# A routed attention and expert kernel: the first turn's weight sums ahead of its rows in the last pair

## The chip, the cores and the metric

The kernel runs on one core of one Trainium2 chip. The metric is device time in microseconds (us), the median of several runs. TensorE is called PE, VectorE DVE, ScalarE ACT, GpSimd POOL and SyncE SP, as the profile does.

## The reference

Two blocks follow each other. The first is a clustered attention over 4 batches, 8 heads, 768 positions and 64 values a head: each query and key is given to the nearest of 16 centroids of its head, and a query sees only the keys of its own cluster.

```python
q_assign = np.argmax(np.einsum('bhsd,hcd->bhsc', q_n, c_n), axis=-1)
k_assign = np.argmax(np.einsum('bhsd,hcd->bhsc', k_n, c_n), axis=-1)
mask = q_assign[:, :, :, None] == k_assign[:, :, None, :]
scores = np.where(mask, scale * np.matmul(q, k.transpose(0, 1, 3, 2)), -1000000000.0)
attn = np.exp(scores - max) / sum          # cut
attn_out = np.matmul(attn, v)
```

The result, 3072 rows of 512, goes through a layer of 8 experts, one expert for each row:

```python
logits = x @ w_gate
expert_idx = np.argmax(logits, axis=1)
gate_w = probs[np.arange(N), expert_idx]   # probs: softmax of logits
for e in range(E):                         # rows of expert e
    h = np.maximum(x_e @ w1[e], 0.0)       # w1[e]: 512 x 1024
    y_e = h @ w2[e]                        # w2[e]: 1024 x 512
out = gate_w[:, None] * y
```

## The kernel before

**Attention, in pairs of heads.** There are 16 pairs, 0 to 15, four to a batch (HP is 4). A pair has 12 units: two halves of the queries (h) by six blocks of keys (j). In each unit `score` (L433) puts scores in PSUM, first q against k, then the cluster masks MQ and MK as a second matmul into the same place; ACT takes the exponential into a tile A (L445), and for j over 0 DVE adds the A tiles to acc (`add_up`, L451). After the units, `attend` (L457) multiplies A by v, and ACT copies the result to oT (L464).

**Work between the units.** The order on every engine is the order of the program; it is written by hand. `at_pair(n, u, f, ...)` hangs a call of f behind unit u of pair n. Unit 12 is between the two halves of `attend`, unit 13 is after them. In this way hang:

- the masks of the next pair: `similar` (PE, L291), then on DVE `assign0`, `assign1` and `assign2` (L302 to L327, ending in ohT), then `place` on ACT (four writes of mk at L340, four of mq at L337), at unit 11;
- the sums of the pair before: `sum_up` (PE, L480) and `weights_of` (DVE, L489 to L504, the gate logits lgb) at unit 2, `rows` (DVE, L510) and `store` (SP, L517, to x_rows) at unit 4;
- the routing of a finished batch: `gate`, `gate_exp`, `gate_sum`, `choose`, `count` (PE, L592), `number` (DVE), and the scatter of positions by POOL to tokens_of (L607).

**Turns of the expert layer.** A turn is up to 448 rows of one expert. There are 10; the first two (EARLY, 288 rows each) take rows of the first three batches, and are got ready while the last batch is still in attention. The steps of turn 0 are:

- `rank_first` (DVE, L645 to L650): 13 small instructions, which choose the experts of turns 0 and 1;
- `first_turns` (SP): reads the experts' numbers, fetches `sf`, the tokens and their factors (`places`, L712 and L716), and then w1 and w2 of turn 0 (L97 and L105);
- `indices` (DVE, L728 and L729) for turns 0 and 1, `gather` (POOL, L738, three indirect DMAs to xg), `weigh` (DVE, L755, and SP's DMAs to turn_rows, L761), `take` (SP, L771, four DMAs to xs), `turn_rows` (DVE, a transpose to xT, L780), `x_sums` (DVE, four sums xc of xT, at L789);
- `w1_sums` (DVE, the four sums a of w1, also recorded at L789).

The last two are the sums of Strassen's scheme (Winograd's form), in which a 2 x 2 block product takes 7 products.

**Layer 1 of turn 0.** `layer1` (matmuls at L968) does 7 products for each of two halves of the hidden blocks, 14 in all. The first takes a block of w1 and xT, the second A[2] and X[2], the third A[1] and X[1], the fourth blocks of w1 and xT, the fifth A[0] and X[0], the seventh A[3]. Behind each product is a hook, 0 to 13, from which calls in `h1` run. In turn 0 these are the last pair's `sum_up` and `weights_of` and the routing of the last batch. The add that makes h (DVE, L926) reads the fifth product, and the seventh product writes into the same bank. `layer2` (L1088 here) follows.

```python
at_pair(n, 2, sum_up, n - 1)
at_pair(n, 4, rows, n - 1)
at_pair(n, 4, store, n - 1)
```

Of the kernel before, what the change touches and what calls it, by code (L numbers as in the profile page):

```python
# [33 lines left out]
def kernel(  # L34
# [11 lines left out]
    nc = tc.nc  # L46
    B, H, S, D = q.shape
# [120 lines left out]
    with tc.manual_schedule(), ExitStack() as actx:  # L168
# [596 lines left out]
        def take(s):  # L765

            g = GR[s]
            T, C = g["T"], g["C"]
            g["xs"] = xp.tile([P, T_MAX // Q4, P], F32, name="xs")
            for r in range(HP):  # L770
                nc.sync.dma_start(  # L771
                    out=g["xs"][Q4 * r : Q4 * (r + 1), 0:C, :],
                    in_=g_d[s][0:T, P * r : P * (r + 1)].rearrange("(c t) d -> t c d", t=Q4),
                )
# [49 lines left out]
        def at_pair(n, u, f, *a):  # L824
            AT.setdefault((n, u), []).append(lambda: f(*a))
# [8 lines left out]
        for b in range(B - 1):  # L834
            n = HP * (b + 1)
# [8 lines left out]
            at_pair(n, 2, weights_of, n - 1)  # L844
        n = HP * (B - 1)
        slots = range(len(EARLY))
        at_pair(n + 1, 4, rank_first)

        def first_turns():
            for s in slots:  # L850
# [3 lines left out]
            GR[0]["w1"] = fetch1(GR[0]["e"], wa)  # L854
            GR[0]["w2"] = fetch2(GR[0]["e"], wa)

        at_pair(n + 1, 6, first_turns)
        for s in slots:
            at_pair(n + 1, 13, indices, s)
        at_pair(n + 2, 6, gather, 0)  # L860
        at_pair(n + 2, 13, weigh, 0)
        at_pair(n + 3, 1, take, 0)
        at_pair(n + 3, 4, turn_rows, 0)
        at_pair(n + 3, 6, x_sums, 0)
        at_pair(n + 3, 9, w1_sums, 0, (2, 1), nc.vector)
        at_pair(n + 3, 13, w1_sums, 0, (0, 3), nc.vector)

        def between(n, u):
            for f in AT.pop((n, u), ()):
# [24 lines left out]
    with tc.manual_schedule(), ExitStack() as ectx:  # L894
# [125 lines left out]
        def pairs_of(s):  # L1020


            return GR[s]["T"] // (2 * P) if s else 0

        def h_sums(s):

            g = GR[s]
            g["H"] = []
            for p in range(pairs_of(s)):
                c0 = 2 * P * p  # L1030
                h = g["h"]
                a11, a21 = h[:, 0:4, c0 : c0 + P], h[:, 0:4, c0 + P : c0 + 2 * P]
                a12, a22 = h[:, 4:8, c0 : c0 + P], h[:, 4:8, c0 + P : c0 + 2 * P]
                t = [hpool.tile([P, 4, P], F32, name=f"hs{i}") for i in range(4)]
                V = nc.vector
                strassen(V, t[2], a11, a21, ALU.subtract)
                strassen(V, t[0], a21, a22, ALU.add)
                strassen(V, t[1], t[0], a11, ALU.subtract)
                strassen(V, t[3], a12, t[1], ALU.subtract)
                g["H"].append((a11, a12, a22, t))  # L1040
# [116 lines left out]
        n = NPAIR  # L1157
        last = NS - 1

        def first_weights(s):  # L1160
            if s >= len(EARLY):
                expert(s)
            GR[s]["w1"] = fetch1(GR[s]["e"], (wa, wb)[s % 2])

        def second_weights(s):
            GR[s]["w2"] = fetch2(GR[s]["e"], (wa, wb)[s % 2])

        for s in range(NS):
            h1, h2 = {}, {}

            def at(d, i, f, *a):
                d.setdefault(i, []).append(lambda: f(*a))

            if s == 0:
                at(h1, 2, sum_up, n - 1)
                at(h1, 2, weights_of, n - 1)
                at(h1, 3, gate, B - 1)
                at(h1, 3, gate_exp, B - 1)
                at(h1, 5, gate_sum, B - 1)
                at(h1, 5, choose, B - 1)  # L1180
                at(h1, 8, count, B - 1)
                at(h1, 9, number, B - 1)
                at(h1, 11, rows, n - 1)
                at(h1, 11, store, n - 1)
                at(h1, 12, rank_all)
                at(h2, 0, rank_rest)
                at(h2, 3, places, 2)
                at(h2, 3, first_weights, 2)
                at(h2, 5, places, 3)
                at(h2, 7, indices, 2)  # L1190
                at(h2, 7, gather, 2)
            if s == 3:
                at(h1, 12, ask)
                at(h2, 4, answer)
            if s < last:
                if s == 0:
                    first_weights(1)
                elif s > 1:
                    take(s + 1)
                if s == 1:  # L1200
                    at(h1, 6, weigh, 2)
                    at(h1, 7, take, 2)
                    at(h1, 8, second_weights, 2)
                else:
                    second_weights(s + 1)
                if 0 < s <= last - 2:
                    at(h2, 0, first_weights, s + 2)

                if 0 < s <= last - 3:
                    at(h2, 1, places, s + 3)  # L1210

                if s == 0:
                    when = ((h2, 1), (h2, 2), (h2, 5), (h2, 6), (h2, 7), (h2, 7))
                elif s == 1:
                    when = ((h1, 9), (h1, 12), (h2, 2), (h2, 3), (h2, 6), (h2, 6))
                else:
                    when = ((h1, 9), (h1, 10), (h2, 1), (h2, 2), (h2, 2), (h2, 5))
                if GR[s + 1]["T"] >= 2 * P:
                    for (h, i), f, a in zip(when, (w1_sums,) * 4 + (w2_sums,) * 2, (2, 1, 0, 3, 2, 0)):
                        at(h, i, f, s + 1, (a,), nc.vector)  # L1220
                at(h2, 1 if s == 1 else 3, turn_rows, s + 1)
                if GR[s + 1]["T"] >= 2 * P:
                    at(h2, 1 if s == 1 else 4, x_sums, s + 1)
            if s == 0:
                at(h1, 2, gather, 1)
                at(h1, 8, weigh, 1, slice(0, 1))
                at(h1, 11, weigh, 1, slice(1, 2))
                at(h1, 12, weigh, 1, slice(2, 3))
                at(h1, 12, take, 1)
            elif s + 2 <= last:  # L1230
                at(h1, 5 if s == 2 else 4, indices, s + 2)
                at(h1, 5 if s == 2 else 4, gather, s + 2)
                at(h2, 6 if s == 1 else 4, weigh, s + 2)
            if pairs_of(s):
                at(h1, 4, w2_sums, s, (1,), nc.vector)

                at(h1, 5 if s == 1 else 6, w2_sums, s, (3,), nc.vector)
            if s == last - 1:

                at(h1, 4, nc.gpsimd.drain)  # L1240
            (layer1 if GR[s]["T"] >= 2 * P else few_columns)(s, h1)
            h_sums(s)
            layer2(s, h2)
# [271 lines left out]
```

## Time and profile before

| what | value |
| --- | --- |
| median of 3 runs | 660.87 us (659.3 to 662.08) |
| the profiled execution | 659.27 us, span 657.5 us |
| PE busy | 644.2 us, 98% of the span |
| DVE busy | 490.0 us, 75% |
| ACT busy | 338.8 us, 52% |
| POOL busy | 130.8 us, 20% |
| granted PE clock | 0.998 |
| first score matmul of pair 13, 14, 15 | 268.96, 288.84, 310.37 us |
| first matmul of the seeds before layer 1 of turn 0 | 329.47 us |
| first matmul of layer 2 of turn 0 | 347.20 us |

The profile is of one execution. Times of the trace count from the start of the span. An instruction of the timeline is given as start, duration, engine, line, operation, what it writes and reads, and in brackets how long the engine stood idle before it and for what. A matmul's end is modelled, so its start is the firmer number.

### The profile page before, as it was taken

The page shows a single profiled execution, that of the slowest core. Times are in us where ns is not written, and L with a number is a line of the kernel's source. Part 1 is how long each engine was busy: PE and PEld are TensorE (multiplying, and loading weights), DVE is VectorE, ACT ScalarE, POOL GpSimd, SP SyncE. Part 2 cuts the span into 40 slices and gives each one's busy share as a digit, 9 for nine tenths or more (in the row PEclk, how much of TensorE's full clock was granted, in tenths as well). Part 3 has the DMA queues.
Part 4 walks back from the last instruction along what each step waited for, and adds up shares of the span by engine and source line. Part 5 has one row for each costly group of instructions (what it writes and reads, how often), then busy time and mean ns, then how long its engine had stood idle before and what let it go on. Part 6 is the DMA issues. An engine that isn't in the chain of part 4 may idle for free.

```text
span 657.5 us, 11491 instructions
## 1 busy us (share of the span) xinstructions
PE 644.2 (98%) x4252; PEld 423.3 (64%) x4252; DVE 490.0 (75%) x845; ACT 338.8 (52%) x584; POOL 130.8 (20%) x166
## 2 busy tenths in 40 slices
PE   8999999999999999999999999999999999999996
PEld 4444544455444454544484979989797987869773
DVE  6988888998889988989887997888869365572300
ACT  4677878768878777867532333333231331323210
POOL 4500000022000300041103522324240422140010
PEclk9999999999999999999999999999999999999999
DMA  7663455443355433347475587776684835614010
GB/s 150 150 120 68 76 94 97 72 80 68 73 97 98 74 76 72 72 132 227 117 273 156 187 314 264 252 275 211 249 307 170 273 138 165 233 74 173 7 49 19
DMA packets 189760, 95.38 MB, mean 145 GB/s; under 512 B 152895, under 2 KB 171839, under 8 KB 188416
## 3 DMA queue, kind: packets, MB, share of 16 engines
q1 hardware_dynamic: 184624, 81.56, 45.2%
q0 software_dynamic: 4928, 12.97, 6.1%
q8 instruction: 35, 0.57, 0.4%
q14 instruction: 29, 0.24, 0.1%
q10 hardware_dynamic: 144, 0.03, 0.0%
HBM read 74.10 MB, written 20.70 MB: 144 GB/s over the span
## 4 chain that ended last, share of the span: by engine, by line
PE 80%; issue 10%; DVE 5%; POOL 2%; ACT 1%; DMA 1%; POOLq 0%; DVEq 0%; ACTq 0%
PE sps L433 20%; PE mps L457 16%; PE bank L968 10%; PE sbank L968 8%; PE bank L1069 7%; PE bank L1088 7%; PE sbank L1069 6%; PE mps L480 2%; PE mps L291 1%; PE bank L937 1%; DMA xg<-x_rows,gi 1%; DVE xT L780 1%; POOL tokens_of L607 1%; DVE acc L451 1%; DVE a L789 1%
## 5 line engine op out<-in xcount | busy, mean ns | idle before, releaser
L445 ACT ACTIVATE A<-sps 128x768 f32<-128x768 f32 x192 | 152.1, 814 | 30.0 <-PE sps L433 29.4
L433 PE MATMUL sps<-qT,kT 64*128 64x384 f32 x768 | 158.9, 492 | 0.0
L451 DVE TENSOR_TENSOR acc<-acc,A 128x768 f32<-128x768 f32 x128 | 121.4, 948 | 11.4 <-ACT A L445 2.9
L457 PE MATMUL mps<-A,v_in 128*64 128x384 f32 x768 | 127.4, 488 | 0.0
L433 PEld LDWEIGHTS sps<-qT,kT 64*128 64x128 f32 x768 | 66.8, 187 | 52.2 <-issue 48.4
L457 PEld LDWEIGHTS mps<-A,v_in 128*64 128x64 f32 x768 | 53.7, 137 | 70.6 <-issue 62.9
L1043 POOL DMA_INDIRECT out_dram<-z,si x30 | 47.7, 1590 | 196.0 <-DVE z L926 167.2
L607 POOL DMA_INDIRECT tokens_of<-tg,pos_i x24 | 27.5, 1147 | 270.5 <-DVE pos_i L605 264.4
L433 PE MATMUL sps<-mq,mk 64*128 64x384 bf16 x384 | 64.9, 323 | 3.1 <-ACT mq L337 1.3
L1088 PE MATMUL bank<-w,h 128*128 128x512 f32 (+2 forms) x224 | 64.4, 596 | 0.0
L340 ACT ACTIVATE mk<-ohT,kscn,ksc 32x384 bf16<-32x384 bf16 x60 | 42.0, 700 | 40.5 <-DVE ohT L327 39.7
L968 PE MATMUL bank<-xT,w 128*128 128x144 f32 (+4 forms) x288 | 47.7, 309 | 0.0
L738 POOL DMA_INDIRECT xg<-x_rows,gi x30 | 38.4, 1280 | 47.0 <-DVE si L729 16.4
L968 PE MATMUL sbank<-xc,a 128*128 128x144 f32 (+4 forms) x288 | 47.7, 309 | 0.0
L1088 PEld LDWEIGHTS bank<-w,h 128*128 128x128 f32 (+2 forms) x224 | 24.6, 151 | 32.5 <-issue 32.3
L968 PEld LDWEIGHTS bank<-xT,w 128*128 128x128 f32 x288 | 43.8, 190 | 2.6 <-issue 2.2
L451 DVE TENSOR_TENSOR acc<-A 128x768 f32<-128x768 f32 x32 | 30.4, 952 | 19.2 <-ACT A L445 19.1
L968 PEld LDWEIGHTS sbank<-xc,a 128*128 128x128 f32 x288 | 43.4, 190 | 0.0
L926 DVE TENSOR_TENSOR h<-sbank,p 128x288 f32<-128x288 f32 (+4 forms) x18 | 9.2, 514 | 45.7 <-PE sbank L968 45.5
L433 PEld LDWEIGHTS <-mk 64*128 64x128 bf16 x384 | 19.9, 94 | 29.0 <-DVE mk L383 2.6
L986 ACT ACTIVATE h<-h 128x288 f32<-128x288 f32 (+4 forms) x36 | 17.6, 488 | 38.1 <-DVE h L926 38.1
L755 DVE TENSOR_TENSOR xw<-xg,sf 128x256 f32<-128x256 f32 (+2 forms) x60 | 32.8, 606 | 0.9 <-DMA xg<-x_rows,gi 0.6
(216 smaller groups left out, 900.5 us busy)
## 6 DMA issues: line engine op xcount, KB each, us to landing
w<-in_moe_w_dram SPq DMA_DIRECT2D x20, 2048.0 KB, 10.7
v_in<-in_v_dram SPq DMA_DIRECT2D x32, 192.0 KB, 2.5
x_rows<-x SPq DMA_DIRECT2D x64, 96.0 KB, 2.4
turn_rows<-xw SPq DMA_DIRECT2D x23, 256.0 KB, 2.0
q_in<-in_q_dram SPq DMA_DIRECT2D x60, 96.0 KB, 3.2
k_in<-in_k_dram SPq DMA_DIRECT2D x60, 96.0 KB, 3.2
xs<-turn_rows SPq DMA_DIRECT2D x16, 144.0 KB, 2.8
xs<-turn_rows SPq DMA_DIRECT2D x8, 208.0 KB, 4.2
```

The costliest lines, as they stand in the source:

```text
L340: nc.scalar.activation(dst, src, AF.Identity, bias=less, scale=big)
L433: nc.tensor.matmul(SP[n, h, j][:, a, 0:HS], lhsT=kt[rows, j * P : (j + 1) * P], rhs=qt[rows, h * HS : (h + 1) * HS], start=first, stop=not ...
L445: nc.scalar.activation(A[n, h, j], ps[:, :, 0:HS], AF.Exp, scale=D**-0.5)
L451: nc.vector.tensor_tensor(ACC[n, h], first, A[n, h, j], op=ALU.add)
L457: nc.tensor.matmul(O[n, h][D * a : D * (a + 1), 0:HS], lhsT=VIN[n][:, a, j, :], rhs=A[n, h, j][:, a, :], start=(j == 0), stop=(j == NQ - 1),)
L607: ins = nc.gpsimd.indirect_dma_start(out=t_d[:, :], out_offset=bass.IndirectOffsetOnAxis(ap=pos_i[:, i : i + 1], axis=0), in_=tg[:, b, i, ...
L738: nc.gpsimd.indirect_dma_start(out=xg[0:m], out_offset=None, in_=x_d[0:rows_in, :], in_offset=bass.IndirectOffsetOnAxis(ap=g["gi"][0:m, j ...
L755: nc.vector.tensor_tensor(xw[0:m, :, :, d2 * a : d2 * (a + 1)], xg[0:m].rearrange("p (r a d b) -> p a r b d", r=HP, a=2, b=DB)[:, a], g["s ...
L968: nc.tensor.matmul(ps[:, f * T2 : (f + 1) * T2], lhsT=w[:, k, (2 * j + f) * P : (2 * j + f + 1) * P], rhs=x[:, k, :], start=first and f + ...
L1043: ins = nc.gpsimd.indirect_dma_start(out=out[:, :], out_offset=bass.IndirectOffsetOnAxis(ap=GR[s]["si"][0:rows, j : j + 1], axis=0), in_=z ...
L1069: nc.tensor.matmul(ps[:, 0:H], lhsT=x[:, k, :], rhs=y[:, k, :], start=first and k == 0, stop=k == 3, skip_group_check=not first,)
L1088: nc.tensor.matmul(ps[i * m : (i + 1) * m, :], lhsT=h[:, f, j * P : j * P + m], rhs=w[:, f, :], start=(k == 0), stop=(k == FB // n - 1),)
```

## The change

n is 12 here, so that n + 1 to n + 3 are pairs 13 to 15. `rank_first` and `first_turns` go from units 4 and 6 of pair 13 to its units 9 and 11. `indices` goes from behind pair 13 to unit 2 of pair 14. `weigh` and `take` go from behind pair 14 and unit 1 of pair 15 to units 11 and 13 of pair 14. In pair 15 the four weight sums, which ran in two groups at units 9 and 13, run one each at units 1 to 4; `turn_rows` and `x_sums` go from units 4 and 6 to 6 and 7. In layer 1 of turn 0, `sum_up`, `weights_of`, `gate` and `gate_exp` move one hook later. No instruction is added or removed.

```diff
-        at_pair(n + 1, 4, rank_first)
+        at_pair(n + 1, 9, rank_first)
...
-        at_pair(n + 1, 6, first_turns)
+        at_pair(n + 1, 11, first_turns)
         for s in slots:
-            at_pair(n + 1, 13, indices, s)
+            at_pair(n + 2, 2, indices, s)
         at_pair(n + 2, 6, gather, 0)
-        at_pair(n + 2, 13, weigh, 0)
-        at_pair(n + 3, 1, take, 0)
-        at_pair(n + 3, 4, turn_rows, 0)
-        at_pair(n + 3, 6, x_sums, 0)
-        at_pair(n + 3, 9, w1_sums, 0, (2, 1), nc.vector)
-        at_pair(n + 3, 13, w1_sums, 0, (0, 3), nc.vector)
+        at_pair(n + 2, 11, weigh, 0)
+        at_pair(n + 2, 13, take, 0)
+
+        for u, i in enumerate((2, 1, 0, 3)):
+            at_pair(n + 3, u + 1, w1_sums, 0, (i,), nc.vector)
+        at_pair(n + 3, 6, turn_rows, 0)
+        at_pair(n + 3, 7, x_sums, 0)
...
-                at(h1, 2, sum_up, n - 1)
-                at(h1, 2, weights_of, n - 1)
-                at(h1, 3, gate, B - 1)
-                at(h1, 3, gate_exp, B - 1)
+                at(h1, 3, sum_up, n - 1)
+                at(h1, 3, weights_of, n - 1)
+                at(h1, 4, gate, B - 1)
+                at(h1, 4, gate_exp, B - 1)
```

## The prediction

> **What bounds the kernel now.** The page's first part says that TensorE (PE) is busy 98% of the span, so only time in which PE stands or is slowed can be won.
>
> ```profile
> PE 644.2 (98%) x4252; PEld 423.3 (64%) x4252; DVE 490.0 (75%) x845; ACT 338.8 (52%) x584; POOL 130.8 (20%) x166
> ```
>
> Next I cut the span at the first score matmul of pairs 12 to 15 and at the first matmul of layer 1 and layer 2 of turn 0 (found in PE's timeline), and asked for busy time by stretch: pair 13, pair 14, pair 15, layer 1 of turn 0, layer 2 of turn 0.
>
> ```profile
> 268.96:288.84 19.88, 19.88 (x156) 9.77 (x154) 18.21 (x45) 11.90 (x18) 6.77 (x6) 1.00 0.21 45
> 288.84:310.37 21.53, 20.21 (x154) 9.89 (x152) 19.49 (x37) 17.47 (x27) 4.58 (x4) 1.00 0.76 254
> 310.37:329.47 19.10, 19.10 (x146) 9.41 (x145) 15.88 (x27) 11.70 (x17) 2.26 (x2) 1.00 0.40 100
> 329.47:347.20 17.73, 16.76 (x144) 15.13 (x143) 14.69 (x37) 6.08 (x16) 2.04 (x3) 1.00 0.68 253
> 347.20:362.98 15.78, 15.78 (x50) 6.41 (x49) 11.27 (x31) 3.07 (x6) 5.52 (x6) 1.00 0.68 199
> ```
>
> The first figure is the stretch, then PE, weight loads, VectorE (DVE), ScalarE (ACT), GpSimd. Pair 15 has no "similar" matmuls, which take 0.65 in pair 14, so pair 14 should last 19.10 + 0.65 = 19.75: it loses **1.78 us**. Layer 1 is 14 products of 0.98, the seeds 0.66, the summing 1.02 and the count 0.05, 15.45 in all: it loses **2.28 us**. The waits of PE name both places (first the pairs, then layer 1):
>
> ```profile
> PE sps L433 <- ACT mq L337: 1.3, 2, 1.1
> PE sbank L968 <- DVE h L926: 0.7, 1, 0.7
> PE mps L592 <- DVE last L586: 0.2, 1, 0.2
> ```
>
> After 360 us PE's waits sum to 1.5 us, so time won here should be kept. Last, the timeline behind the first wait:
>
> ```profile
> 279.60 0.11 DVE L645 TENSOR_TENSOR c<-run,first_place 1x8 f32<-1x8 f32 x1
> 281.70 0.16 DVE L650 CAST xe<-xe_f 1x2 int32<-1x2 f32 x1
> 286.82 0.58 DVE L327 STREAM_TRANSPOSE ohT<-oh 128x384 bf16<-128x384 bf16 x1
> 287.43 2.85 ACT L340 ACTIVATE mk<-ohT,kscn,ksc 32x384 bf16<-32x384 bf16 x4 [5.56 <-DVE ohT L327]
> 290.86 0.32 PE L433 MATMUL sps<-mq,mk 64*128 64x384 bf16 x1 [1.10 <-ACT mq L337]
> ```
>
> rank_first stands in DVE's queue ahead of the mask chain (sim to ohT) of pair 14; ohT ends at 287.4, ACT writes four mk and then mq, and PE wants the second mq at 289.6 and gets it at 291.39. And behind the second loss, in pair 15 and layer 1:
>
> ```profile
> 322.41 1.38 DVE L780 STREAM_TRANSPOSE xT<-xs 128x1152 f32<-128x1152 f32 x1 [2.48 <-DMA xs<-turn_rows]
> 333.59 1.22 DVE L789 TENSOR_TENSOR a<-w 128x1024 f32<-128x1024 f32 x1
> 334.73 1.22 DVE L789 TENSOR_TENSOR a<-w,a 128x1024 f32<-128x1024 f32 x1
> 335.86 0.38 DVE L489 STREAM_TRANSPOSE slt<-mps 128x192 f32<-128x192 f32 x1
> 338.24 0.46 DVE L926 TENSOR_TENSOR h<-sbank,p 128x288 f32<-128x288 f32 x1 [0.22 <-PE bank L968]
> ```
>
> DVE stands 2.48 us for the turn's rows, and is then late: its last adds end at 333.7, while PE's summing (L480) has begun at 333.16, and the first layer-1 add comes at 338.24, for which the last product waits.
>
> [...] the trace has 1.22 us for a weight sum[...] layer 1 shows 0.97 us idle where 2.28 is lost, so I use starts, and DVE's queue is its program order. [...] gathers issued while w1 and w2 were in flight landed after 6.2 to 8.1 us, later ones after 4.1 to 5.0.
>
> **The change, part by part.** Times are on the scale of the trace.
>
> *rank_first from unit 4 to unit 9 of pair 13.* 13 small DVE instructions, 279.60 to 281.78, 2.18 us, go behind the mask chain. ohT then ends at 285.2 and ACT has the second mq at 289.15, ahead of PE's 289.6: the wait goes, **gain 1.78**. Late next is DVE itself: the last adds of pair 13 still end at 291.3, where pair 14's summing begins at 291.5, so 0 to 0.2 may return.
>
> *What follows from a later rank.* It ends at 289.33 instead of 281.86. SP's loads of the expert numbers were at 282.5, behind the store of rows; SP spent 2.55 us to its first sf read, waited 2.4 us for tokens_of (then done), and took 3.43 us from the first sf to the second weight fetch. So sf issues at 291.95 to 294.35, w1 at 294.9 and w2 at 295.4, 4.5 us later than now. Nothing else stands in SP's queue in between: the rows of pair 12 go before, those of pair 13 come at 299. With the landings of the trace, sf is there at 296.0 (1.5 to 1.8 us), w1 at 302 (7.4), w2 at 311.5 (16.1).
>
> *indices from (13, 13) to (14, 2).* Eight instructions, 0.63 us, enter DVE's pair 14. DVE comes to them at 293.1 + 3.3 (two acc, the weights_of) = 296.4, so 0.4 us of cover remains over sf. A wait there would hold every acc and the next mask chain behind it. The chain ends at 297.0 + 8.4 = 305.4; ACT gives the second mq at 309.3, PE wants it at 308.6 + 0.75 = 309.3: no cover left, 0 to 0.3.
>
> *gather, weigh, take.* The gathers keep their place; POOL gets gi at 296.5, 3 us later than now, and issues at 296.6 to 300. With 6.2 to 8.1 us they land by 308; weigh reaches DVE at 297.0 + 12.3 = 309.3. Cover 1.3 us. weigh at unit 11 and take at 13 stand in the queues of DVE and SP exactly where they stood, since pair 14 prepares no pair 16: nothing, and their seven DMAs move with weigh, 1.0 us earlier.
>
> *Weight sums first, rows later, in pair 15.* The same nine DVE instructions. Four sums of 1.2 us now fill the wait for xs (landed at 321.4), w1 having landed at 302. DVE's list from 312.6: ten acc at 0.98, four sums 4.85, weights_of 1.35, x 0.95, xT 1.35, xc 1.75, ends at 332.6 at most (332.2 by single starts), xT at 325.6 and xc at 328.2. PE starts layer 1 at 327.7 (329.47 - 1.78), wants X[2] at 329.3 and all of xc by 330.3: in time.
>
> *sum_up and weights_of one hook later, gate too.* PE reaches the summing after four products, at 332.3, with the adds done: the 0.6 lost there goes. DVE runs weights_of at 333.4 to 334.9 and the add for h at once, so the 0.9 at the last product goes. But the count keeps its hook, 5 products after the summing instead of 6. From the end of the summing, 333.4, to "last" I sum 1.5 + 0.5 + 0.7 + 1.05 (Exp, u2, the second add) + 2.2 = 5.95 us, where PE needs 5.0: a wait of up to 0.95 where there is 0.2 to 0.4. Layer 1 thus gains 0.9 by this sum and 2.2 at most if all waits vanish. The rows of that sum were taken with DVE behind; I take the middle, **1.6**.
>
> Sum: 1.78 + 1.6 = 3.4, bounds 0 and 4.0. The profiled execution took 659.27 us (span 657.5 and 1.8 around it), so 655.9; the median of the runs shown, 660.87, is 1.6 above it, so **657.5** on that scale. Their scatter is 659.3 to 662.08.
>
> **Rivals.**
> 1. *The count becomes the wait.* Gain 1.78 + 0.9, with 0 to 0.5 back from the thin covers: 2.2 to 2.7, or 658.2 to 658.7. For it: the latencies are measured. Against: the chain may shorten where DVE isn't behind.
> 2. *The turn's data come late (slower).* If the gathers queue behind the 4 MB of weights, they land after w2's 311.5 and weigh holds DVE from 309.3, with the ten acc of pair 15 and the summing behind it. Every us after 309.3 is a us of layer 1. Slower than before from a landing after 312.7 on, and by over 0.5% from 316; at 317 the time is 657.5 + 7.7 = 665.2. For it: 4.5 us later weights. Against: the gathers of now landed in the midst of the same 4 MB.
> 3. *No real move.* Parts of the edit leave the queues as they are (weigh, take). But rank_first and the sums do change places in DVE's queue; left without gain only if pair 14's wait returns at pair 15 (cover 0): 660.9.
>
> **How the numbers follow.** A difference of 0.5%, 3.3 us, is about what a measurement of this kernel can tell from no change. Both losses go: 0.52, faster, 657.5, own range 656.5 to 657.6. Rivals 1 and 3: 0.36, within 0.5%. Rival 2: 0.12. The range runs from the bound of 4.0 with the scatter of the runs, 654.8, to rival 3 with the same, 661.6.
>
> **What would show it.** In pair 14 no PE wait for mq, and 19.8 us from start to start; rank_first after ohT; the gi instructions without a DMA wait at about 296.4; xT without one; layer 1 at 16.1 us (16.8 under rival 1, with a wait of the count, L592, on "last"). Wrong: a DVE wait on sf or xg of over 1 us, a PE wait for mq in pair 15, or layer 1 over 17.5.

## The result and the profile after

| | before | after |
| --- | --- | --- |
| median (11 runs each) | 660.87 us (659.3 to 662.08) | 658.29 us (656.73 to 659.77) |
| the profiled execution | 659.27 us, span 657.5 | 657.44 us, span 655.7 |

The ratio of after to before is 0.9967, with a 95% interval of 0.9956 to 0.9979: 2.2 us gained (1.4 to 2.9), where 3.4 was forecast. In the changed program the lines behind the edit are one higher (L926 is L927, L968 is L969).

The busy time by stretch, cut at the same matmuls (pair 14, pair 15, layer 1 of turn 0), has the stretch and its length first, then PE, weight loads, DVE, ACT and POOL:

```profile
288.37:308.64 20.27, 20.27 (x154) 9.79 (x152) 18.72 (x39) 14.77 (x22) 4.47 (x4) 1.00 0.70 251
308.64:327.74 19.10, 19.10 (x147) 9.41 (x145) 18.77 (x29) 12.15 (x18) 2.27 (x2) 1.00 0.53 121
327.74:344.36 16.62, 16.03 (x143) 14.99 (x142) 11.83 (x35) 5.99 (x16) 2.05 (x3) 1.00 0.72 270
```

Pair 14 lost 1.26 us of its 21.53, pair 15 is as long as before with DVE 2.9 us busier in it, layer 1 lost 1.11 us of its 17.73. PE's waits from pair 12 to the start of turn 1 now are one line. The wait for mq and the one for the add of h are gone; the one at the count has grown from 0.2:

```profile
PE mps L592 <- DVE last L586: 0.6, 1, 0.6
```

The timeline of the kernel after, from pair 13 to layer 1, has the start, the duration and, in brackets, the idle time before. These are the lines that answer to those shown of before:

```profile
284.13 0.58 DVE L327 STREAM_TRANSPOSE ohT<-oh 128x384 bf16<-128x384 bf16 x1
284.75 2.85 ACT L340 ACTIVATE mk<-ohT,kscn,ksc 32x384 bf16<-32x384 bf16 x4 [3.35 <-DVE ohT L327]
286.54 0.15 DVE L645 TENSOR_TENSOR c<-run,first_place 1x8 f32<-1x8 f32 x1
291.52 0.94 DVE L277 STREAM_TRANSPOSE kT<-k_in 128x768 f32<-128x768 f32 x1
292.51 0.84 PE L291 MATMUL mps<-kT,cT 128*32 128x384 f32 x4
296.74 0.15 DVE L728 SCALAR_TENSOR_TENSOR gi<-sf 32x1 int32<-32x1 f32 x1 [0.62 <-DMA sf<-tokens_of]
323.66 1.37 DVE L780 STREAM_TRANSPOSE xT<-xs 128x1152 f32<-128x1152 f32 x1
333.66 0.38 DVE L489 STREAM_TRANSPOSE slt<-mps 128x192 f32<-128x192 f32 x1 [2.01 <-PE mps L480]
335.02 0.45 DVE L927 TENSOR_TENSOR h<-sbank,p 128x288 f32<-128x288 f32 x1
339.10 0.17 DVE L586 CAST last<-pr 128x8 bf16<-128x8 f32 x1
```

ohT comes 2.2 us earlier against PE and rank_first starts behind it. xT waits for nothing. DVE now stands ready for the summing (2.01 us idle) where before it was late. Two lines were not in the forecast: PE's similar takes kT only at 292.51, just as DVE has turned it, and the last gi stands 0.62 us for sf.

Against the first matmul of pair 14 the kernel after is 2.37 us ahead at the first matmul of layer 2 of turn 0. It does not keep all of it: it gives back 0.40 in layer 2 of turn 2 and 0.48 in layer 1 of turn 3, and at the end of the span 1.36 is left.

### The profile page after: what moved, and what is told of

Read it like the earlier page. It is cut to its first block, busy times and chain, and to the rows that moved or that the text cites. A ratio compares the mean times of both kernels' runs of the same rounds, so it can differ in the third digit from the quotient of the medians.

```text
span 655.7 us, 11490 instructions
## 1 busy us (share of the span) xinstructions
PE 643.5 (98%) x4252; PEld 423.0 (65%) x4252; DVE 489.5 (75%) x845; ACT 338.3 (52%) x584; POOL 133.0 (20%) x166
## 4 chain that ended last, share of the span: by engine, by line
PE 94%; DVE 4%; issue 0%; ACT 0%; POOL 0%; POOLq 0%; DVEq 0%; ACTq 0%
PE sps L433 24%; PE mps L457 19%; PE bank L969 12%; PE bank L1089 10%; PE sbank L969 9%; PE bank L1070 7%; PE sbank L1070 6%; PE mps L480 3%; PE mps L291 2%; PE bank L938 1%; DVE xT L780 1%; DVE a L789 1%; DVE v L789 1%; PE sps L356 0%; PE sps L226 0%
## 5 line engine op out<-in xcount | busy, mean ns | idle before, releaser
L738 POOL DMA_INDIRECT xg<-x_rows,gi x30 | 40.3, 1343 | 45.8 <-DVE si L729 16.5
L969 PE MATMUL sbank<-xc,a 128*128 128x144 f32 (+4 forms) x288 | 47.9, 309 | 0.2 <-ACT sbank L1002 0.2
L969 PE MATMUL bank<-xT,w 128*128 128x144 f32 (+4 forms) x288 | 47.6, 308 | 0.0
L969 PEld LDWEIGHTS bank<-xT,w 128*128 128x128 f32 x288 | 43.8, 190 | 2.3 <-issue 1.9
L969 PEld LDWEIGHTS sbank<-xc,a 128*128 128x128 f32 x288 | 43.3, 190 | 0.7 <-ACT sbank L1002 0.4
L927 DVE TENSOR_TENSOR h<-sbank,p 128x288 f32<-128x288 f32 (+4 forms) x18 | 9.2, 513 | 45.3 <-PE sbank L969 43.9
```

What stands on the lines that cost most here:

```text
L738: nc.gpsimd.indirect_dma_start(out=xg[0:m], out_offset=None, in_=x_d[0:rows_in, :], in_offset=bass.IndirectOffsetOnAxis(ap=g["gi"][0:m, j ...
L969: nc.tensor.matmul(ps[:, f * T2 : (f + 1) * T2], lhsT=w[:, k, (2 * j + f) * P : (2 * j + f + 1) * P], rhs=x[:, k, :], start=first and f + ...
```

## The experiments

All traces are cut at the same matmuls. "Through layer 1" is the time from the first matmul of pair 14 to the first of layer 2 of turn 0, the whole place of the change. The ratios are to the kernel before on the same chip; "turn 1" is layer 1 of turn 1.

| kernel | pair 14 | pair 15 | layer 1 | through layer 1 | turn 1 | ratio (95% interval) |
| --- | --- | --- | --- | --- | --- | --- |
| before | 21.53 | 19.10 | 17.73 | 58.36 | 14.58 | |
| before_again | 21.52 | 19.10 | 17.91 | 58.53 | 13.76 | |
| after | 20.27 | 19.10 | 16.62 | 55.99 | 14.50 | 0.9967 (0.9956 to 0.9979) |
| after_again | 20.28 | 19.36 | 16.62 | 56.26 | 15.20 | 0.9975 (0.9967 to 0.9984) |
| rank_only | 20.27 | 19.95 | 18.25 | 58.47 | 13.88 | 0.9995 (0.9983 to 1.0007) |
| sums_only | 21.52 | 19.10 | 16.44 | 57.06 | 14.72 | 0.9988 (0.9979 to 0.9997) |
| hooks_only | 21.52 | 19.10 | 17.06 | 57.68 | 14.79 | 0.9990 (0.9980 to 1.0000) |
| rank_back | 21.46 | 19.09 | 16.63 | 57.18 | 14.82 | 0.9994 (0.9983 to 1.0004) |
| old_hooks | 20.26 | 19.10 | 16.77 | 56.13 | 14.69 | 0.9976 (0.9967 to 0.9984) |
| count_later | 20.28 | 19.10 | 15.87 | 55.25 | 14.71 | 0.9965 (0.9952 to 0.9979) |
| indices_later | 20.26 | 19.10 | 16.63 | 55.99 | 14.38 | 0.9969 (0.9958 to 0.9981) |
| later_both | 20.28 | 19.10 | 15.87 | 55.25 | 14.91 | 0.9949 (0.9935 to 0.9963) |
| rank_last_count | 19.74 | 19.10 | 15.87 | 54.71 | 14.84 | 0.9940 (0.9927 to 0.9953) |
| rows1_earlier | 19.74 | 19.10 | 16.00 | 54.84 | 15.27 | 0.9949 (0.9930 to 0.9968) |

The intervals are 0.6 to 1.3 us to either side, so parts of a microsecond are told apart by the stretches, not by the ratios. A stretch is from one execution.

### The change in its parts

**The later rank alone** (rank_only, from the kernel before):

```diff
-        at_pair(n + 1, 4, rank_first)
+        at_pair(n + 1, 9, rank_first)
-        at_pair(n + 1, 6, first_turns)
+        at_pair(n + 1, 11, first_turns)
         for s in slots:
-            at_pair(n + 1, 13, indices, s)
+            at_pair(n + 2, 2, indices, s)
```

> The kernel before with only the later rank: rank_first at unit 9, first_turns at unit 11 of pair 13, indices at unit 2 of pair 14. Theory (two separate delays on VectorE): pair 14 shortens from 21.53 to about 20.27 us as in the changed kernel (mask wait gone, a wait of similar for kT of about 0.5 us new), layer 1 of turn 0 stays near 17.7 us or grows by up to 0.5 because PE comes earlier; gain 0.8 to 1.3 us, ratio 0.998 to 0.999. Rival (the rank makes all of it): gain 2.2 us, ratio 0.9967, layer 1 at 16.6. Rival (late data cost what the rank gives): pair 15 or layer 1 longer by over 1 us, ratio 1.000.

Pair 14 gains its 1.26 us, and then pair 15 is 0.85 and layer 1 0.52 us longer: through layer 1 nothing is won in this execution (58.47 against 58.36). The ratio's interval holds both no gain and the 0.998 to 0.999 of the theory. The timeline of rank_only shows where the gain went; DVE, SP and PE in order of time:

```profile
294.08 0.33 SPq L716 DMA_DIRECT2D sf<-tokens_of  x1
294.59 0.35 SPq L97 DMA_DIRECT2D w<-in_moe_w_dram  x1
298.34 0.15 DVE L728 SCALAR_TENSOR_TENSOR gi<-sf 32x1 int32<-32x1 f32 x1 [1.68 <-DMA sf<-tokens_of]
310.26 0.32 PE L433 MATMUL sps<-mq,mk 64*128 64x384 bf16 x1 [0.17 <-ACT mq L337]
310.75 3.29 DVE L755 TENSOR_TENSOR xw<-xg,sf 128x256 f32<-128x256 f32 x6
310.80 0.32 PE L433 MATMUL sps<-mq,mk 64*128 64x384 bf16 x1 [0.21 <-ACT mq L337]
322.59 1.38 DVE L780 STREAM_TRANSPOSE xT<-xs 128x1152 f32<-128x1152 f32 x1 [2.27 <-DMA xs<-turn_rows]
```

The last rows of sf, 1.2 KB, freed DVE only 4.3 us after their issue; in before such fetches landed in 1.5 to 1.8 us. DVE, standing for them, held the next mask chain, and the wait for mq came back one pair later. The rival of late data is right in kind, though neither stretch alone is longer by the 1 us that it asked for.

The packet records of the trace point to what held the data. Turn 1's sf is 288 packets of 40 bytes, of which 286 had ended by 295.21 us; the other two started at 297.12, and a 16 KB fetch of the instruction queue ran from 294.85 to 297.13. The same fetch and two packets are in all seven traced kernels with this timing of the rank:

| | instruction fetch | last two packets start | DVE's wait on sf |
| --- | --- | --- | --- |
| after | 294.43 to 295.53 | 295.52 | 0.62 |
| after_again | 294.11 to 295.83 | 295.81 | 1.07 |
| rank_only | 294.85 to 297.13 | 297.12 | 1.68 |
| old_hooks | 294.55 to 295.95 | 295.93 | 0.69 |
| count_later | 294.73 to 295.61 | 295.59 | none |
| indices_later | 294.07 to 295.04 | 295.03 | none, reader later |
| later_both | 294.67 to 295.80 | 295.79 | none, reader later |

In before the fetch came at 299.40, long after sf, and in rank_last_count at 293.91 to 294.82, ahead of it: no packets stood there. The fetch itself took 0.88 to 0.91 us in the seven traces in which it met no sf, and 0.88 to 2.28 in these. The weights are issued within half a microsecond of it, and whether they made it longer was not tested. Nor is the whole delay explained: the last completion came 1.13 to 1.15 us after the end of the two packets, where it comes after 0.33 to 0.34 in the traces without a hold.

**The new order of pair 15 alone** (sums_only, from before):

```diff
-        at_pair(n + 2, 13, weigh, 0)
-        at_pair(n + 3, 1, take, 0)
-        at_pair(n + 3, 4, turn_rows, 0)
-        at_pair(n + 3, 6, x_sums, 0)
-        at_pair(n + 3, 9, w1_sums, 0, (2, 1), nc.vector)
-        at_pair(n + 3, 13, w1_sums, 0, (0, 3), nc.vector)
+        at_pair(n + 2, 11, weigh, 0)
+        at_pair(n + 2, 13, take, 0)
+        for u, i in enumerate((2, 1, 0, 3)):
+            at_pair(n + 3, u + 1, w1_sums, 0, (i,), nc.vector)
+        at_pair(n + 3, 6, turn_rows, 0)
+        at_pair(n + 3, 7, x_sums, 0)
```

> The kernel before with only the new order of pair 15 (weight sums at units 1 to 4, rows and x sums at 6 and 7). Theory: pair 14 stays at 21.5 us; VectorE's last adds end some 3.4 us after PE enters layer 1 instead of 4.2, the four sums of w1 are done, so summing and last product don't wait; layer 1 of turn 0 falls from 17.73 to about 16.2 us with a wait of 0.5 at the count; gain 1.5 us, ratio 0.9977. Rival (only idle time of VectorE is filled, the later hooks make the gain of layer 1): layer 1 at 17.4 or more, ratio 0.9995.

Layer 1 falls by 1.29 us to 16.44, and PE's wait for the add of h is gone. The theory holds in the stretch; 16.2 was a little low, and the ratio shows less gain than the 0.9977 expected. The later hooks are not needed for this.

**The later hooks alone** (hooks_only, from before):

```diff
-                at(h1, 2, sum_up, n - 1)
-                at(h1, 2, weights_of, n - 1)
-                at(h1, 3, gate, B - 1)
-                at(h1, 3, gate_exp, B - 1)
+                at(h1, 3, sum_up, n - 1)
+                at(h1, 3, weights_of, n - 1)
+                at(h1, 4, gate, B - 1)
+                at(h1, 4, gate_exp, B - 1)
```

> The kernel before with only sum_up, weights_of, gate and gate_exp one hook later in layer 1 of turn 0. Theory: the wait at the summing (0.6 us) goes as PE comes 1 us later to it, but VectorE is still in the w1 sums until 6.5 us after PE's entry, so the add of h and the last product wait nearly as before and the count 0.3 to 0.5; layer 1 from 17.73 to about 16.9 us, gain 0.8, ratio 0.9988. Rival (the hooks make all of layer 1's gain): 16.6 us, gain 1.1, ratio 0.9983. Rival (the hooks cost, since the count has a product less of cover): 17.7 us or more.

Layer 1 falls by 0.67 us to 17.06. PE's wait for the add of h goes from 0.7 to 0.2, and the one at the count rises from 0.2 to 0.6. So the hooks make part of what the new order makes too, by another way: they give DVE a product more of time.

**The change without the later rank** (rank_back, from after):

```diff
-        at_pair(n + 1, 9, rank_first)
+        at_pair(n + 1, 4, rank_first)
-        at_pair(n + 1, 11, first_turns)
+        at_pair(n + 1, 6, first_turns)
-            at_pair(n + 2, 2, indices, s)
+            at_pair(n + 1, 13, indices, s)
```

> The changed kernel with rank_first, first_turns and indices back at their old units. Theory: pair 14 again 21.5 us with PE's waits for mq; layer 1 of turn 0 at 16.3 to 16.6 us since VectorE is not later against PE; gain over the kernel before 1.1 to 1.4 us, ratio 0.998. Rival (the rank makes all of it): ratio 0.9995 or more.

Pair 14 is at 21.46 again and layer 1 at 16.63. Through layer 1 it gains 1.18 us of 58.36. The measured ratio of 0.9994 is less gain than that, though its interval reaches 1.1 us. The ratio alone would fit the rival, that the rank makes all of it; what speaks against the rival is the stretch, layer 1 at 16.63 without the later rank.

**The change with the old hooks** (old_hooks, from after):

```diff
-                at(h1, 3, sum_up, n - 1)
-                at(h1, 3, weights_of, n - 1)
-                at(h1, 4, gate, B - 1)
-                at(h1, 4, gate_exp, B - 1)
+                at(h1, 2, sum_up, n - 1)
+                at(h1, 2, weights_of, n - 1)
+                at(h1, 3, gate, B - 1)
+                at(h1, 3, gate_exp, B - 1)
```

> The changed kernel with sum_up, weights_of, gate and gate_exp at their old hooks 2 and 3 (later rank and new order of pair 15 kept). Theory: the new order alone had layer 1 at 15.8 us with 0.2 us of wait at the count, since the count keeps six products of cover; here VectorE's last adds end 0.2 us after PE comes to the summing, so 16.0 us; ratio 0.6 us or 0.001 below the changed kernel. Rival (the later hooks are needed once the rank is later, because the adds end too late for the summing): 16.6 us or more.

Layer 1 is 16.77 us. With the later rank, the adds end as PE comes to the summing: its 24 matmuls took 1.44 us from their first start to the start of the next product, where they take 1.11 in after; the count still waited 0.2. The expectation mixed two scales. Its 15.8 us for sums_only counts from the first product, without the seeds of 0.65 us; on the scale of the table that is 16.44, and with the 0.2 us of the theory 16.64. So the theory's step is nearly right, its gain over after was not, and on one scale the rival's 16.6 does not differ from it. What is shown is that the hooks earn 0.15 us once the rank is late.

Through layer 1 the rank alone gains nothing (-0.11) and the rest 1.18, but both 2.37. That does not prove that the parts need each other, for rank_only's execution had the longest wait on sf, and the wait moves DVE's queue: weigh starts 20.79, 21.25 and 21.84 us behind the first matmul of pair 14 in after, after_again and rank_only, with waits of 0.62, 1.07 and 1.68, which is 20.16 to 20.18 without the wait in each. In before it starts at 21.52. In the old order of pair 15 xT, which stands for xs, follows weigh by 11.8 to 12.2 us (before, before_again, hooks_only, rank_only). My estimate from these figures is that without the wait rank_only's rows would be ready some 1.4 us earlier than in before (21.52 less 20.16), about as much as pair 14 gains. So the hold may account for most of what was lost. The later rank with the indices later and the old order of pair 15 would tell; it was not run.

### The change again, and the kernel before again

after_again and before_again are the two kernels unaltered, so there is no edit to show.

> The changed kernel, unaltered, timed and profiled a second time. Theory: pair 14 at 20.27 us, layer 1 of turn 0 at 16.6 us, both set by the program's order, in this execution too; the 0.4 and 0.5 us given back in layer 2 of turn 2 and layer 1 of turn 3 are the landing of one weight fetch and come and go (between 0 and 1.5 us). Ratio 0.996 to 0.998. Rival (the give-back is part of the change): 0.9 us again in turns 2 and 3.

> The kernel before, unaltered, profiled a second time. Theory: pair 14 at 21.5 us and layer 1 of turn 0 at 17.7 us again, since VectorE's queue sets both; layer 2 of turn 2 between 12.1 and 13.6 us, as the weight fetch lands. Rival (the wait for mq was a chance of one execution): pair 14 at under 21 us.

Pair 14 and layer 1 are set by the order: 20.28 and 16.62, 21.52 and 17.91. The wait for mq was no chance. In after_again the last gi waited 1.07 us for sf, and pair 15 is 0.26 us longer for it. In layer 2 of turn 2, 1.33 us was given back this time (13.43 us against 12.10), with one wait of 2.9 us on DVE for a weight fetch (1.4 in before). That stretch was between 12.5 and 13.6 us also in after, hooks_only, indices_later, later_both and rows1_earlier, and 12.1 in the eight other profiles, both of before among them. No part of the change picks it out: it is in hooks_only and not in rank_back, which has the same hooks. Why the fetch lands late was not found, and with two profiles of before a link to the change is not excluded.

### What the change left

**The count a hook later** (count_later, from after):

```diff
-                at(h1, 8, count, B - 1)
-                at(h1, 9, number, B - 1)
+                at(h1, 9, count, B - 1)
+                at(h1, 10, number, B - 1)
```

> The changed kernel with count at hook 9 and number at hook 10 instead of 8 and 9. Theory (the count became the wait): the 0.6 us wait of PE on 'last' goes with a product more of cover, layer 1 from 16.6 to about 15.9 us. Rival (number and the scatter to tokens_of a product later come back in turn 1): layer 1 of turn 1 grows from 14.5 us by 0.5 or more.

Layer 1 is 15.87 us, 0.4 above its matmuls, and no PE wait is left in it. Layer 1 of turn 1 did not grow by 0.5. The count had become the wait.

**The indices later** (indices_later, from after):

```diff
-        for s in slots:
-            at_pair(n + 2, 2, indices, s)
+        at_pair(n + 2, 4, indices, 0)
+        at_pair(n + 2, 9, indices, 1)
```

> The changed kernel with the indices of turn 0 at unit 4 and of turn 1 at unit 9 of pair 14 instead of both at unit 2. Theory (the fetch of the last rows of sf lands late behind the weights, and VectorE, waiting for it, holds the mask chain): no wait on sf, ohT of pair 15 0.6 us earlier, no mask wait in pair 15 whatever the landing; pair 14 stays 20.27 us because of kT; in an execution where the landing is early no gain, else up to 0.9 us. Ratio to before 0.0005 to 0.001 below the changed kernel's. Rival (the later gather makes weigh late): wait on xg of over 1 us, layer 1 longer.

DVE has no wait on sf any more, though the last two packets were held here too. (They started at 295.03 us, as the instruction fetch ended at 295.04; the expectation had put the hold down to the weights.) In this pair of executions that is worth nothing (55.99 in both), since after's own 0.62 us had found cover; against after_again's pair 15 it is worth 0.26.

**Both** (later_both, from after):

```diff
-        for s in slots:
-            at_pair(n + 2, 2, indices, s)
+        at_pair(n + 2, 4, indices, 0)
+        at_pair(n + 2, 9, indices, 1)
...
-                at(h1, 8, count, B - 1)
-                at(h1, 9, number, B - 1)
+                at(h1, 9, count, B - 1)
+                at(h1, 10, number, B - 1)
```

> The changed kernel with both repairs: the indices at units 4 and 9 of pair 14, count at hook 9 and number at hook 10. Theory: the two add up, pair 14 20.27, pair 15 19.10 and layer 1 of turn 0 15.9 us in every execution; gain over the kernel before 2.7 to 3.2 us, ratio about 0.996. Rival (one hides the other): ratio 0.997.

The stretches add up as expected. Its ratio, 0.9949, is lower than the 0.996 expected.

**The rank behind the turns of q and k** (rank_last_count, from later_both):

```diff
-        at_pair(n + 1, 9, rank_first)
+        at_pair(n + 1, 13, rank_first)
-        at_pair(n + 1, 11, first_turns)
+        at_pair(n + 1, 13, first_turns)
-        at_pair(n + 2, 4, indices, 0)
+        at_pair(n + 2, 5, indices, 0)
```

> The changed kernel with rank_first and first_turns at unit 13 of pair 13, behind the turns of q and k, the indices at units 5 and 9 of pair 14, count at hook 9 and number at hook 10. Theory (similar waits for kT, which the rank holds up by 2.2 us): kT comes 2.2 us earlier, pair 14 falls from 20.27 to 19.75 us, layer 1 at 15.9; gain 3.2 to 3.7 us, ratio about 0.995. Rival (late data, as in the prediction: sf, weights and gathers are 2 us later again): VectorE waits for xg before weigh by 1 us or more and its last adds are that much late, layer 1 of turn 0 at 16.9 us or more, which eats the 0.5.

The busy time by stretch of rank_last_count has the same three stretches:

```profile
288.47:308.21 19.74, 19.74 (x155) 9.68 (x153) 18.70 (x47) 15.06 (x23) 5.27 (x4) 1.00 0.48 173
308.21:327.31 19.10, 19.10 (x147) 9.42 (x145) 18.16 (x28) 11.96 (x18) 5.53 (x3) 1.00 0.75 208
327.31:343.18 15.87, 15.87 (x144) 15.00 (x143) 12.41 (x36) 5.99 (x16) 1.58 (x2) 1.00 0.75 283
```

PE is busy for the whole of all three. Pair 14 has come to the 19.75 us that its matmuls need, so the 0.52 left there was the wait for kT. Its timeline shows the price on the data side, now small:

```profile
289.66 0.94 DVE L277 STREAM_TRANSPOSE kT<-k_in 128x768 f32<-128x768 f32 x1
290.52 0.11 DVE L645 TENSOR_TENSOR c<-run,first_place 1x8 f32<-1x8 f32 x1
309.33 3.44 DVE L755 TENSOR_TENSOR xw<-xg,sf 128x256 f32<-128x256 f32 x6 [0.70 <-DMA xg<-x_rows,gi]
```

kT is turned 1.9 us earlier than in after. weigh waits 0.70 us for the gathered rows, which stays hidden. At 0.9940 (3.1 to 4.8 us gained) and a median of 655.65 us against 659.5, it beats both kernels, before and after: its interval, 0.9927 to 0.9953, lies clear of after's 0.9956 to 0.9979, though each was measured beside before and not beside the other.

**Turn 1's last rows earlier** (rows1_earlier, from rank_last_count):

```diff
-                at(h1, 12, weigh, 1, slice(2, 3))
+                at(h1, 11, weigh, 1, slice(2, 3))
```

> The version with the rank last, indices later and count later, and the last part of turn 1's weigh at hook 11 of layer 1 of turn 0 instead of 12, ahead of rank_all on VectorE. Theory (when layer 1 of turn 0 gets shorter, turn 1's rows become the next thing late: VectorE stands 3.6 us for xs before xT, and PE waits in turn 1's layer 1): xs lands some 2 us earlier, the wait for xs falls to about 2 us, layer 1 of turn 1 goes from 14.8 to 13.9 us; ratio 0.001 below that version, 0.993. Rival (the weights of turn 1 in flight set the landing of xs, not weigh): xs no earlier, layer 1 of turn 1 stays at 14.4 to 14.9 us. Rival (rank_all a us later delays the fetches of turns 2 and 3): layer 2 of turn 2 longer by 1 us.

The theory falls. DVE was done with the rows at 345.5 us, in rank_last_count, which ran 0.6 earlier, at 347.5. But SP's queue shows why that brings nothing:

```profile
343.43 3.90 SPq L517 DMA_DIRECT2D x_rows<-x  x4
347.43 1.35 SPq L761 DMA_DIRECT2D turn_rows<-xw  x2
351.09 1.81 SPq L771 DMA_DIRECT2D xs<-turn_rows  x4
```

The four stores of the last pair's rows, 3.9 us of issuing, stand ahead of turn_rows in SP's queue, so that its last issue ends 5.04 us behind the start of layer 2, and 5.05 in rank_last_count. xs is issued at 7.3 us, in rank_last_count at 6.9, and layer 1 of turn 1 was 15.27 us. The first rival forecast that xs would be no earlier, which came; the 0.4 us by which xs is later here lie behind that issue, and what makes them was not shown. This kernel was also 1.5 us longer in layer 2 of turn 2, as the second rival forecast, and 1.2 in layer 1 of turn 3; but layer 2 of turn 2 was that long in other kernels too, where rank_all had not moved, so this does not show that rival right.

## Why the prediction was right and where not

**Right in kind.** Both losses were where the stretches put them, both went as the chain of steps said, and nothing took their place at full size. The kernel is faster, and the time, 658.29, lies in the range. But the gain is 2.2 us and not 3.4, so it falls within 0.5%, which had the smaller chance of the two, and outside the 656.5 to 657.6 of the leading case. The bounds of the range do not come out of the numbers given for them: 4.0 off and 1.6 of scatter below, and 1.2 of scatter above rival 3, make 655.3 to 662.1 instead of 654.8 to 661.6, and 658.29 lies in both.

**The rank in pair 14: 1.78 forecast, 1.26 measured.** The wait for mq is gone as forecast, ohT at 284.7 (285.2 less the 0.47 us by which this execution ran earlier). The step that failed is "late next": I named the last adds and allowed 0 to 0.2 us, and did not follow what else stands behind the rank in DVE's queue and has a reader on PE. The turn of k does: similar wants kT 1.0 us after the start of the summing, and got it 0.5 us late. rank_last_count, with the turns ahead of the rank, has the full 1.79 (21.53 to 19.74).

**Late data.** I took sf's landing from the trace of before, 1.5 to 1.8 us, and got 0.4 us of cover. From issue to the reader it was 3.2 us in after, 3.7 in after_again and 4.3 in rank_only. The step that failed is to carry a landing over to another moment: in before an instruction fetch was 9 us away from sf, and in the new order, in which it also came some 5 us earlier, it met sf. The wait on DVE, none to 1.7 us where the indices stand at unit 2, cost PE nothing to 0.85. after_again's 1.07 is over the 1 us that the prediction named as a sign of being wrong. Of the slower rival only so much came; weigh, which started at 309.16 us without a wait, and the ten adds of pair 15 were not held by gathers behind the weights in after.

**Layer 1: 1.6 forecast, 1.11 measured.** The sum by rows said 0.9, with a count wait of up to 0.95, and I took the middle between that and the whole 2.2. The count waited 0.59 and count_later shows that it was worth 0.75 (16.62 to 15.87). Rival 1, with its 0.9 and its wait at the count, was nearer, and its 658.2 to 658.7 holds the measured time. The reason I gave for the middle, that the chain may be shorter when DVE isn't behind, was worth 0.2 and not 0.7.

**Pair 15.** The DVE list was right to 0.1 us: ten adds ending at 331.65, that is 332.1 on the scale of the prediction, against 332.2 to 332.6.

**After layer 1.** I held that what is won is kept, since PE waits 1.5 us in all after 360 us. Three places there took some back, not all of them in every trace. Layer 1 of turn 1 was 14.4 to 15.3 us in the eleven profiles whose layer 1 of turn 0 was shorter than before, 14.8 in the mean, and 13.8 to 14.6 in the other three, 14.1 in the mean. Its rows come later there: xT, which stands for xs, starts 11.3 to 12.2 us behind the start of layer 2 in the eleven and 10.7 to 11.1 in the three. In rows1_earlier 3.90 us of stores stand ahead of turn_rows in SP's queue, which has a part in this; why the rows are later was not shown. Layer 2 of turn 2 was 12.1 us in both traces of before and 12.1 to 13.6 in the others.

**The sum.** 1.26 and 1.11 make 2.37 through layer 1 in the traced execution, and the measured 2.2 (1.4 to 2.9) agrees with it in size. That it is the same time isn't shown, and part of the agreement may be luck. From pair 14 to the end the two traces of before took 368.69 and 368.08 us and the two of after 367.33 and 368.57, which keeps 0.4 of it in the mean. The traced executions of before were 1.6 and 1.3 us faster than the medians beside them. Where the untraced ones spend that time isn't known.

## What to carry to other kernels

When an instruction is moved back in a queue that runs in program order, as DVE's did here (the rank ran from 279.60 to 281.86 us, ahead of sim at 282.65, in before, and from 286.54 to 288.79, behind ohT at 284.13, in after), list everything that it now stands ahead of, and look up the first reader of each on the engine that sets the time: the wait that was removed can come back at the next of them, smaller, as it did here at the turn of k. When a part gains nothing alone, look whether its execution met a wait of its own before you conclude that the parts need each other. A landing time read from a trace need not hold in another order: sf landed in 1.5 to 1.8 us in before, and in the new order its reader had it 3.2 to 4.3 us after the issue where it stood for it. A reader in a critical queue wants cover for more than the landing of before, and if it isn't urgent itself, a later place.

## What the runs showed of the hardware

In these traces a small fetch stood while a fetch of instructions ran. In the seven traces above, two of 288 packets started only when a 16 KB instruction fetch of 0.88 to 2.28 us ended, to within 0.02 us, while the other 286 had ended 0.4 to 1.9 us earlier. The fetch of the last 32 rows of sf, 32 packets of 40 bytes, has sixteen completions: in before all came from 291.14 to 291.35 us, and in after fifteen came from 294.81 to 295.03 and one at 296.71. My estimate from these counts is two packets a completion, so that the late completion is that of the two packets that stood. Why they stood was not shown; the packet records name no engine.
